# A planner's dependence between matmuls of one sum, and its figures for transfers, in a fused attention and expert kernel

## The chip, the cores and the metric

One core of a Trainium2 chip runs the whole program in one launch. The metric is the device time of an execution in microseconds (us), lower being better. The figure for a kernel is the median of its runs.

## The reference, cut to what matters

Three stages follow each other: attention that keeps the 32 largest scores of a row, a dense mixture of four experts, and a gated product of two linear maps. All is float32.

```python
# q, k, v: (2, 8, 576, 64)
scores = q @ k.T / sqrt(64)
kth    = 32nd largest of each row of scores
attn   = softmax(where(scores >= kth, scores, -1e9))
x      = (attn @ v) as (1152, 512)
p      = domain_probs / (sum(domain_probs) + 1e-9)          # (1152, 4)
x      = sum over e of p[:, e] * (relu(x @ w1[e]) @ w2[e])   # w1 512x1024, w2 1024x512
out    = ((x @ w_a) * (x @ w_b)) @ w_out                     # 512x1536, 1536x512
```

## The kernel before, in words

**Tiles and groups.** The 1152 rows make nine tiles of 128 rows (the ninth mixes the last 64 rows of both batches). They are taken in four groups of 1, 2, 3 and 3 tiles (`SIZES`). A group passes attention in four pairs of heads, so attention has 36 steps, one for a tile and a pair. In a step TensorE makes the scores of two heads, ScalarE copies them out (L821), VectorE finds the 32 largest with four `max` and three `match_replace` passes for each head (L842, L850), POOL and ScalarE turn them into weights (L867 to L892), TensorE transposes these (`weigh`, `turn`) and, after the last tile of the pair, multiplies by v. ScalarE and VectorE write the result into `xs` (L984, L986) as a rounded part and a remainder.

**Experts.** The first group goes through `plain` in full float32. The others go through `experts`: `first` makes one 128-wide piece of the hidden layer as a sum of four steps, one for each pair of heads (`a`), `second` one tile of the output as a sum over hidden pieces. A step is three matmuls, since operands are split in two parts. Each step is an operation of its own that names the step before it as `last`. Sums of `first`, of `second` and of `plain` use three banks of PSUM (`ms`). ScalarE and VectorE empty a hidden piece (L1077, L1081), and VectorE adds an expert's output (L1106). Weights come by loads of 512 KB (L518 is the line of all loads); ScalarE rounds them (L1007), POOL or VectorE makes the remainder (L1008).

**Gated stage.** `combine` makes sums of quarters of x, and `gated` does the three products, in the way of Strassen, with sums that are one operation each (`product`), emptied by L1387.

**q's halves.** From the second group on, `queries` splits q in two parts and transposes both at once. Each half of the partitions then holds one part; ScalarE copies that out (L726), and two DMAs within SBUF fetch the other half into `qb` (`big<-big`). For groups with the mixed tile, `qm` is filled in the same way (L736, `qm<-qm`).

**The order of work.** Nothing in the source fixes the order. `Plan.add` collects operations with an engine, an estimated duration (`hold`), a `lag` until others can see its end, a key, operations to wait for and tiles. `order` plays the program forward on a clock: each engine takes the ready operation with the lowest key whose tiles have a slot. It gives the instruction order of every engine, the DMA queue on SyncE (SP) included. `best` does so 42 times with random lateness added, replays every order in `rerun` with other random lateness, and keeps the order with the lowest mean. Only this order goes into the program; on the chip each engine runs its list in order and waits on semaphores for what an instruction really needs. Keys put scores, then attention, ahead of expert work, which is numbered from 1000 upwards in the order of the source.

In `order` an operation that ends is seen 45 ns later by others, and 130 ns later by TensorE (`SEEN`, `SEEN_PE`); TensorE's own `lag` is 165 ns (`tensor`). A load counts as landed after `ISSUE` 500 ns, its bytes at 320 bytes a ns on one shared line (`GBS`), and `LAND` ns.

Of the kernel before, what the change touches and what calls it, by code (L numbers as in the profile page):

```python
# [9 lines left out]
F32 = mybir.dt.float32  # L10
# [79 lines left out]
SEEN, SEEN_PE = 45, 130  # L90
COLD, COLD_END = 1.7, 46e3

OTHER = {"DVE": "POOL", "POOL": "DVE"}
RATES = {"DVE": 0.65, "POOL": 0.5}


def contend(engine, hold, other, left):
# [1 line left out]
    a, b = RATES[engine], RATES[other]  # L99
    t = min(hold / a, left / b)  # L100
    return t + hold - a * t, t + left - b * t
ISSUE, LAND, GBS, LANES = 500, 2100, 320.0, 8

# [5 lines left out]
class Plan:  # L111
# [37 lines left out]
    def rerun(self, got, draw):  # L149

        free, end, dma, users = {}, {}, 0.0, {}
        last, runs = 0.0, {}
        for op in got:
            t = free.get(op.engine, 0.0)
            for w in op.waits:
                t = max(t, end[id(w)] + (SEEN_PE if op.engine == "PE" else SEEN))

            for b in op.tiles:
                u = users.get(id(b))
                if u is None:  # L160
                    u = users[id(b)] = [max([self.freed.get(k, 0.0) for k in b.slots.cells(b.slot)] or [0.0])]
                t = max(t, u[0] + (SEEN_PE if op.engine == "PE" else SEEN))
            hold = op.hold * COLD if op.engine == "PE" and t < COLD_END else op.hold
            if op.engine == "SP":
                free["SP"] = t + ISSUE
                dma = max(dma, t + ISSUE) + op.nbytes / GBS
                e = dma + LAND + draw.uniform(0.0, LATE_DMA)
            else:
                if op.port:
                    other = OTHER[op.engine]  # L170
                    y = runs.get(other)
                    if y is not None and free[other] > t:
                        hold, left = contend(op.engine, hold, other, free[other] - t)
                        end[id(y)] += t + left - free[other]
                        free[other] = t + left
                if op.engine in OTHER:
                    runs[op.engine] = op if op.port else None
                free[op.engine] = t + hold
                e = t + hold + op.lag + (draw.uniform(0.0, LATE_ENGINE) if op.engine != "PE" else 0.0)
            end[id(op)] = e  # L180
            last = max(last, e)
            for b in op.tiles:
                k = (b.slots.name, b.slot)
                self.freed[k] = max(self.freed.get(k, 0.0), e)
        self.freed.clear()
        return last

    def order(self):
# [12 lines left out]
        late, ready, free, events, tick = {}, {}, {}, [], 0  # L201
# [16 lines left out]
        queue, now, done = [(op.since, -1, None) for op in self.ops if op.since], 0.0, []  # L218
# [28 lines left out]
        def pick(engine):  # L247
# [6 lines left out]
            while ready_:  # L254
                item = heapq.heappop(ready_)
                op = item[2]

                y = runs.get(OTHER[engine]) if BLOCK and op.port else None
                ok = y is None or free[y.engine] <= now
# [15 lines left out]
        while len(done) < len(self.ops):  # L275
            moved = False
            for engine in free:
                if free[engine] > now:
                    continue
                if engine == "SP" and len(lanes) >= LANES and lanes[-LANES] > now:  # L280
                    continue
                op = pick(engine)
                if op is None:
                    continue
                moved = True
                for t in op.tiles:
                    if t.slot is None:
                        t.slot = place(t)
                        t.slots.free.discard(t.slot)
                        t.slots.next += 1  # L290
                op.start = now
                done.append(op)
                if engine == "SP":
                    free[engine] = now + ISSUE
                    dma_free = max(dma_free, now + ISSUE) + op.nbytes / GBS
                    end = dma_free + LAND
                    lanes.append(end)
                else:
                    hold = op.hold * COLD if engine == "PE" and now < COLD_END else op.hold
                    if op.port:  # L300
                        other = OTHER[engine]
                        y = runs.get(other)
                        if y is not None and free[other] > now:
                            hold, left = contend(engine, hold, other, free[other] - now)
                            y.fin += now + left - free[other]
                            free[other] = now + left
                            heapq.heappush(queue, (y.fin, y.n, y))
                            heapq.heappush(queue, (free[other], -1, None))
                    if engine in OTHER:
                        runs[engine] = op if op.port else None  # L310
                    free[engine] = now + hold
                    end = now + hold + op.lag + op.late
                op.fin = end
                heapq.heappush(queue, (end, op.n, op))
                heapq.heappush(queue, (free[engine], -1, None))
            if moved:
                continue
            if not queue:
                raise RuntimeError("the plan stands still: " + str([(o.n, o.engine, o.key) for o in self.ops if o.start is None][:8]))
            now = max(now, queue[0][0])  # L320
            while queue and queue[0][0] <= now:
                _, _, op = heapq.heappop(queue)
                if op is None:
                    continue
                if isinstance(op, Buffer):
                    op.slots.free.add(op.slot)
                    continue
                if op.fin > now:
                    continue
                for t in op.tiles:  # L330
                    t.users -= 1
                    if not t.users:
                        heapq.heappush(queue, (now + t.slots.rest, -2 - op.n - 0.1 * op.tiles.index(t), t))
                for a in op.after:
                    a.left -= 1
                    a.at = max(a.at, now + (SEEN_PE if a.engine == "PE" else SEEN))
                    if not a.left:
                        heapq.heappush(late[a.engine], (a.at, a.n, a))
                        heapq.heappush(queue, (a.at, -1, None))
# [37 lines left out]
def body(tc, q, k, v, probs, w1, w2, wa, wb, wo, out):  # L377
# [58 lines left out]
    qm = const("qm", [128, 2, 2, 2, 128], F32R)  # L436
# [78 lines left out]
    def load(dst, src, key, after=(), tiles=(), nbytes=1 << 18, since=0.0):  # L515


        op = plan.add("SP", 0, lambda: nc.sync.dma_start(out=dst(), in_=src()), key, after, tiles, nbytes=nbytes)  # L518
        op.since = since
        return op  # L520
# [182 lines left out]
    def queries(pair, n, key, eng, rqv, tiles, lds):  # L703
# [3 lines left out]
        qa, qb, at = qas.tile(n), qbs.tile(n), atts.tile(key + 0.04)  # L707
# [8 lines left out]
        def turn():  # L716
# [6 lines left out]
        w = m * 128  # L723
        av = lambda: qa.ap[:, 0:2 * w].rearrange("p (j n) -> p j n", j=2)
        bv = lambda: qb.ap[:, 0:2 * w].rearrange("p (j n) -> p j n", j=2)
        e = scalar(2 * w, lambda: nc.scalar.activation(av(), at.ap[:, :, 0:w], AF.Copy), -901, [o], [at, qa])  # L726
        got = [e] + [
            load(lambda r=r: bv()[r * 64:(r + 1) * 64].bitcast(F32), lambda r=r: av()[(1 - r) * 64:(2 - r) * 64].bitcast(F32), -500, [e], [qa, qb], 512 * w)
            for r in range(2)
        ]  # L730
        pair.qd, pair.q = {0: got, 1: got}, [qa, qb]
# [1 line left out]
        if m < T:  # L733
            es_ = [
                scalar(
                    2 * REM, lambda b=b: nc.scalar.activation(  # L736
                        qm[:, :, b, 0, b * REM:(b + 1) * REM], at.ap[:, :, w + b * REM:w + (b + 1) * REM], AF.Copy
                    ), -900, [o] + qm_read[0] + qm_read[1], [at],
                ) for b in range(B)
            ]  # L740
            qm_read[:] = [], []
            pair.md = es_ + [
                load(lambda r=r: qm[r * 64:(r + 1) * 64, :, :, 1].bitcast(F32), lambda r=r: qm[(1 - r) * 64:(2 - r) * 64, :, :, 0].bitcast(F32), -400, es_, (), 1 << 17)
                for r in range(2)
            ]

# [707 lines left out]
    for i in range(FILL):  # L1454
        late = i >= 9
        op = tensor(
            120 if late else 215, lambda: mm(idle.ap[:, 0:256], zeros_[:, 0:128], zeros_[:, 128:384], start=True, stop=True),
            1e9 + i, [blank], [idle],
        )
# [33 lines left out]
```

## Time and profile before

| what | value |
|---|---|
| median of 3 runs | 823.16 us (821.83 to 823.45) |
| the profiled execution's own time | 820.39 us |
| its span, first to last instruction | 818.6 us |
| mean granted TensorE clock | 0.997 |
| busy TensorE (PE) / weight loads (PEld) | 789.1 / 705.0 us |
| busy VectorE (DVE) | 735.3 us |
| busy ScalarE (ACT) / GpSimd (POOL) | 525.0 / 350.7 us |

Busy time is a share of the whole span and hides stages. A matmul's recorded end is modelled and reaches into the next one, so that a mean duration is longer than the distance between starts; the distance of starts is the pace.

### The profile page before, as it was taken

The numbers are of one execution on the slowest core, as the hardware profiler recorded it, in microseconds if no ns is written. First come the engines' busy times: TensorE is split into PE (matmuls) and PEld (weight loads), VectorE is DVE, ScalarE is ACT, GpSimd is POOL, SyncE is SP. The second block draws the span as 40 slices with busy tenths as digits, with TensorE's granted clock in tenths as the row PEclk, the third lists the DMA queues.
The fourth block names the chain that finished last, engine by engine and source line by source line (L and its number), as shares of the span: only waits on it lengthen the run. The fifth ranks groups of instructions, "written<-read, shape, count | busy, mean of one in ns | idle before, by whom it ended". The sixth has DMA issues, their size and how long they took to land.

```text
span 818.6 us, 14468 instructions
## 1 busy us (share of the span) xinstructions
PE 789.1 (96%) x5221; PEld 705.0 (86%) x5221; DVE 735.3 (90%) x1447; ACT 525.0 (64%) x917; POOL 350.7 (43%) x317
## 2 busy tenths in 40 slices
PE   7589999999999999999999999999999999999997
PEld 6467777789899999899999999899989989899996
DVE  7999999999999999999984998888877899997654
ACT  6877887998899989888565667666634533341110
POOL 3524433798898967754121211221313333422120
PEclk9999999999999999999999999999999999999999
DMA  6839988856657462633334555989330412221013
GB/s 209 284 108 318 322 274 236 256 166 213 204 173 205 148 202 91 201 103 104 103 103 155 168 171 181 330 309 316 120 104 24 133 52 103 78 78 52 1 52 116
DMA packets 95511, 134.39 MB, mean 164 GB/s; under 512 B 11344, under 2 KB 69712, under 8 KB 93904
## 3 DMA queue, kind: packets, MB, share of 16 engines
q1 hardware_dynamic: 95440, 133.47, 51.1%
q8 instruction: 41, 0.67, 0.3%
q14 instruction: 30, 0.25, 0.1%
HBM read 115.36 MB, written 13.37 MB: 157 GB/s over the span
## 4 chain that ended last, share of the span: by engine, by line
PE 64%; DVE 26%; ACT 4%; DMA 3%; issue 1%; POOL 1%; SPq 0%; POOLq 0%; ACTq 0%
PE ps L536 61%; DVE low L842 12%; DVE low L850 10%; PE ps L539 2%; DMA raw<-in_moe_w_dram 1%; DVE mid L1081 1%; DMA big<-big 1%; DVE low L1106 1%; DMA low<-in_k_dram 1%; ACT low L892 1%; ACT mid L1007 0%; ACT lowa L821 0%; ACT low L881 0%; DVE rest L1387 0%; POOL low L877 0%
## 5 line engine op out<-in xcount | busy, mean ns | idle before, releaser
L536 PE MATMUL ps<-mid 128*128 128x512 f32 x1092 | 278.4, 394 | 0.0
L536 PEld LDWEIGHTS ps<-mid 128*128 128x128 f32 x1092 | 198.5, 188 | 32.8 <-DVE mid L1081 0.7
L536 PE MATMUL ps<-xs,mid 128*128 128x384 f32 (+1 forms) x1152 | 204.3, 321 | 1.2 <-DVE mid L1081 1.1
L536 PEld LDWEIGHTS ps<-xs,mid 128*128 128x128 f32 x1152 | 185.0, 189 | 9.9 <-DVE mid L1081 2.2
L842 DVE MAX8 low<-low 128x8 f32<-128x576 f32 x216 | 155.0, 749 | 0.1
L1298 POOL TENSOR_TENSOR low<-low 128x512 int32<-128x512 int32 x36 | 52.7, 1464 | 162.1 <-DVE low L1295 119.4
L1008 POOL TENSOR_TENSOR mid<-raw,mid 128x1024 fp32r<-128x1024 f32 x48 | 115.2, 2406 | 8.0 <-ACT mid L1007 6.9
L1007 ACT ACTIVATE mid<-raw 128x1024 fp32r<-128x1024 f32 x96 | 101.7, 1063 | 17.7 <-PE ps L536 16.5
L877 POOL TENSOR_TENSOR low<-lowa,low 128x576 f32<-128x576 f32 x70 | 98.8, 1430 | 29.4 <-ACT low L873 28.4
L850 DVE MATCH_REPLACE8 low<-low 128x576 f32<-128x576 f32 x144 | 106.3, 744 | 0.0
L536 PE MATMUL ps<-xs,big 128*128 128x320 f32 (+1 forms) x576 | 87.8, 297 | 0.1
L536 PEld LDWEIGHTS ps<-xs,big 128*128 128x128 f32 x576 | 81.3, 190 | 2.5 <-DVE low L1387 0.3
L536 PE MATMUL ps<-lowa_again,big 128*128 128x320 f32 (+1 forms) x432 | 66.8, 297 | 1.0 <-ACT rest L1396 0.8
L536 PEld LDWEIGHTS ps<-lowa_again,big 128*128 128x128 f32 x432 | 61.5, 190 | 3.4 <-ACT rest L1396 1.1
L1008 DVE TENSOR_TENSOR mid<-raw,mid 128x1024 fp32r<-128x1024 f32 x48 | 58.9, 1229 | 6.0 <-ACT mid L1007 5.7
L1077 ACT ACTIVATE mid<-ps 128x384 fp32r<-128x384 f32 (+1 forms) x96 | 43.3, 456 | 30.4 <-PE ps L536 27.8
L892 ACT ACTIVATE low<-low 128x576 f32<-128x576 f32 x70 | 51.1, 773 | 16.3 <-DVE low L889 16.1
L539 PE MATMUL ps<-identr,low 128*128 128x128 f32 x360 | 53.4, 283 | 7.3 <-ACT low L892 6.6
L873 ACT ACTIVATE low<-lowa,low 128x576 f32<-128x576 f32 x70 | 52.1, 776 | 11.8 <-POOL low L867 11.8
L539 PEld LDWEIGHTS ps<-identr,low 128*128 128x128 f32 x360 | 42.3, 144 | 19.2 <-ACT low L892 13.4
L1081 DVE SCALAR_TENSOR_TENSOR mid<-ps,mid 128x384 fp32r<-128x384 f32 (+1 forms) x96 | 48.2, 506 | 11.3 <-ACT mid L1077 10.8
L881 ACT ACTIVATE low<-low 128x576 f32<-128x576 f32 x70 | 54.6, 781 | 3.1 <-POOL low L877 3.1
(120 smaller groups left out, 1176.4 us busy)
## 6 DMA issues: line engine op xcount, KB each, us to landing
raw<-in_moe_w_dram SPq DMA_DIRECT2D x122, 512.0 KB, 3.9
big<-kscr SPq DMA_DIRECT2D x20, 576.0 KB, 6.0
low<-in_v_dram SPq DMA_DIRECT2D x24, 256.0 KB, 4.0
low<-in_moe_w_b_dram SPq DMA_DIRECT2D x12, 512.0 KB, 3.7
low<-in_moe_w_a_dram SPq DMA_DIRECT2D x12, 512.0 KB, 4.2
low<-in_moe_w_out_dram SPq DMA_DIRECT2D x12, 512.0 KB, 4.4
wscr<-big SPq DMA_DIRECT2D x6, 1024.0 KB, 7.4
mid<-wscr SPq DMA_DIRECT2D x6, 1024.0 KB, 5.2
```

Source lines behind the costliest of these rows:

```text
L536: nc.tensor.matmul(out, l, r, **kw)
L539: nc.tensor.transpose(out, a, i)
L842: 62 + 1.04 * width, lambda at=at, cs=cs: nc.vector.max(m8v()[:, x, cs], at()), key + 0.02 * r, [done],
L850: lambda at=at, cs=cs: nc.vector.match_replace(out=src[1](), in_to_replace=m8v()[:, x, cs], in_values=at(), imm_value=LOW),
L873: S, lambda x=x, s=s: nc.scalar.activation(ev(x), s.ap, AF.Relu, bias=endv()[:, x, 1:2], scale=-STEEP),
L877: pool_(S), lambda x=x, s=s: nc.gpsimd.tensor_tensor(ev(x), s.ap, ev(x), op=ALU.subtract), ks, [a], [s, ep]
L881: lambda x=x: nc.scalar.activation(ev(x), ev(x), AF.Exp, bias=endv()[:, x, 0:1], scale=scale, accum_out=sums.ap[:, x:x + 1]),
L892: S, lambda x=x: nc.scalar.activation(ev(x), ev(x), AF.Copy, scale=sums.ap[:, x:x + 1]),
L1007: hi = scalar(1024, lambda: nc.scalar.activation(u.ap[:, 0:1024], r.ap, AF.Copy), 500 + s, [ld], [u, r], sbuf=True)
L1008: sub = lambda eng: eng.tensor_tensor(u.ap[:, 1024:2048], r.ap, u.ap[:, 0:1024], op=ALU.subtract)
L1081: lambda h=h, p=p: nc.vector.scalar_tensor_tensor(h.ap[:, n:2 * n], p.ap[:, 0:n], 0.0, h.ap[:, 0:n], op0=ALU.max, op1=ALU.subtract),
L1298: return gpsimd(pool_(512), lambda: nc.gpsimd.tensor_tensor(t().bitcast(I32), fold(c.ap.bitcast(I32)), fold(lowv().bitcast(I32)), op=ALU.a ...
```

## The change

The planner alone changes; operations, tiles, keys and durations stay. In `order`, when a TensorE operation is placed, TensorE operations that wait for it count it as done at once (they can start when the engine is free), and its end no longer tells them; in `rerun` a TensorE operation no longer waits for another TensorE operation's end. `LAND` goes from 2100 to 2700 ns. The bytes that the planner counts for the exchange of q's halves double, for `qb` and for `qm`. `CHAIN` is read nowhere.

```diff
+CHAIN = True
-ISSUE, LAND, GBS, LANES = 500, 2100, 320.0, 8
+ISSUE, LAND, GBS, LANES = 500, 2700, 320.0, 8
...
             for w in op.waits:
-                t = max(t, end[id(w)] + (SEEN_PE if op.engine == "PE" else SEEN))
+                if w.engine != "PE" or op.engine != "PE":
+                    t = max(t, end[id(w)] + (SEEN_PE if op.engine == "PE" else SEEN))
...
                 op.start = now
                 done.append(op)
+                if engine == "PE":
+                    for a in op.after:
+                        if a.engine == "PE":
+                            a.left -= 1
+                            a.at = max(a.at, now)
+                            if not a.left:
+                                heapq.heappush(late["PE"], (a.at, a.n, a))
...
                 for a in op.after:
+                    if a.engine == "PE" and op.engine == "PE":
+                        continue
                     a.left -= 1
...
-            load(lambda r=r: bv()[r * 64:(r + 1) * 64].bitcast(F32), lambda r=r: av()[(1 - r) * 64:(2 - r) * 64].bitcast(F32), -500, [e], [qa, qb], 512 * w)
+            load(lambda r=r: bv()[r * 64:(r + 1) * 64].bitcast(F32), lambda r=r: av()[(1 - r) * 64:(2 - r) * 64].bitcast(F32), -500, [e], [qa, qb], 1024 * w)
...
-                load(lambda r=r: qm[r * 64:(r + 1) * 64, :, :, 1].bitcast(F32), lambda r=r: qm[(1 - r) * 64:(2 - r) * 64, :, :, 0].bitcast(F32), -400, es_, (), 1 << 17)
+                load(lambda r=r: qm[r * 64:(r + 1) * 64, :, :, 1].bitcast(F32), lambda r=r: qm[(1 - r) * 64:(2 - r) * 64, :, :, 0].bitcast(F32), -400, es_, (), 1 << 18)
```

## Rows read from the trace of the kernel before

**Rows 1.** By stretch: length, busy us of PE, PEld, DVE, ACT, POOL, then clock.
```profile
0.00:60.00 60.00, 44.09 (x282) 36.19 (x283) 54.18 (x121) 44.56 (x91) 23.69 (x42) 0.97 0.63 198
60.00:160.00 100.00, 93.89 (x688) 73.20 (x687) 99.89 (x218) 79.65 (x145) 44.62 (x49) 1.00 0.91 278
160.00:293.00 133.00, 131.77 (x1023) 119.32 (x1022) 131.57 (x285) 120.13 (x216) 117.80 (x84) 1.00 0.62 192
...
420.00:600.00 180.00, 180.00 (x979) 163.30 (x978) 150.59 (x236) 110.34 (x168) 38.13 (x26) 1.00 0.63 211
600.00:640.00 40.00, 38.97 (x256) 36.32 (x255) 32.55 (x72) 19.46 (x37) 9.81 (x10) 1.00 0.16 53
```

**Rows 2.** TensorE's instructions in order of time, around 293 us.
```profile
292.92 0.62 PE L539 MATMUL ps<-identr,big 128*128 128x128 f32 x6
293.38 1.82 PE L536 MATMUL ps<-xs,mid 128*128 128x384 f32 x9
```

**Rows 3.** VectorE's instruction that completes the third group's x.
```profile
293.08 0.56 DVE L986 TENSOR_TENSOR xs<-ps,xs 128x384 fp32r<-128x384 f32 x1
```

**Rows 4.** TensorE's instructions in order of time, from 477.8 to 488 us.
```profile
477.80 5.40 PE L536 MATMUL ps<-mid 128*128 128x512 f32 x23
483.04 0.69 PE L536 MATMUL ps<-xs,mid 128*128 128x384 f32 x3
483.56 0.86 PE L536 MATMUL ps<-mid 128*128 128x512 f32 x3
484.25 0.70 PE L536 MATMUL ps<-xs,mid 128*128 128x384 f32 x3
```

**Rows 5.** Who waited for whom, TensorE's matmuls and weight loads, whole span.
```profile
PE ps L536 <- DMA big<-big: 2.9, 3, 1.3
PE ps L536 <- DVE mid L1081: 1.1, 3, 0.4
PEld ps L536 <- DMA big<-big: 3.8, 4, 1.5
PEld ps L536 <- DVE mid L1081: 2.9, 8, 0.6
PEld ps L536 <- DMA raw<-in_moe_w_dram: 0.8, 2, 0.5
```

**Rows 6.** All engines in order of time, one exchange of q's halves.
```profile
149.75 0.82 ACT L726 ACTIVATE big<-ps 128x768 fp32r<-128x768 f32 x1
...
150.60 1.11 SPq L518 DMA_DIRECT2D big<-big  x2
...
156.20 1.17 PE L536 MATMUL ps<-big 128*128 128x288 f32 x7 [1.28 <-DMA big<-big]
```

**Rows 7.** DMA issues: what, count, KB each, median us from issue to landing.
```profile
raw<-in_moe_w_dram SPq DMA_DIRECT2D x122, 512.0 KB, 3.9
...
big<-big SPq DMA_DIRECT2D x16, 128.0 KB, 6.7
...
big<-big SPq DMA_DIRECT2D x8, 192.0 KB, 5.7
```

**Rows 8.** All engines in order of time, the start.
```profile
8.49 0.63 ACT L591 ACTIVATE big<-low 128x512 fp32r<-128x512 f32 x1 [0.72 <-DMA low<-in_k_dram]
...
9.03 0.63 ACT L821 ACTIVATE lowa<-ps 128x576 f32<-128x576 f32 x1
...
9.69 1.50 DVE L842 MAX8 low<-lowa 128x8 f32<-128x576 f32 x2 [2.16 <-ACT lowa L821]
```

**Rows 9.** VectorE's evictions, whole span: count, busy us, mean ns, idle before.
```profile
L1081 DVE SCALAR_TENSOR_TENSOR mid<-ps,mid 128x384 fp32r<-128x384 f32 (+1 forms) x96 | 48.2, 506 | 11.3 <-ACT mid L1077 10.8
L1106 DVE SCALAR_TENSOR_TENSOR low<-ps,pr,low 128x512 f32<-128x512 f32 x44 | 32.6, 743 | 6.1 <-PE ps L536 5.9
```

**Rows 10.** The same groups from 160 to 293 us.
```profile
L1081 DVE SCALAR_TENSOR_TENSOR mid<-ps,mid 128x256 fp32r<-128x256 f32 x31 | 12.7, 414 | 0.4 <-ACT mid L1077 0.3
L1106 DVE SCALAR_TENSOR_TENSOR low<-ps,pr,low 128x512 f32<-128x512 f32 x14 | 10.4, 742 | 0.0
```

## The prediction

> **What bounds the kernel now.** I read the busy time by stretch first [rows 1]. TensorE (PE) is the bound after about 160 us: from 420 to 600 us it is busy all 180.00 us, while VectorE (DVE) has 29 us to spare. Over the whole span it is busy for 789.1 of 818.6 us, so there are 29.5 us in which it stands still, and their places matter: 60.00 - 44.09 = 15.9 us lie before 60 us, 100.00 - 93.89 = 6.1 us between 60 and 160, 133.00 - 131.77 = 1.2 us between 160 and 293, and 1.0 us between 600 and 640. Most of the rest is the tail behind the last matmul. The granted clock is 0.97 before 60 us and 1.00 in the other stretches listed, so the clock has nothing to give.
>
> The early idle time is not TensorE's own fault. DVE, which searches the 32 largest scores, is busy 99.89 of 100 us from 60 to 160 and 131.57 of 133 from 160 to 293 [rows 1]. The two engines meet at 293 us: DVE's L986 begins at 293.08 and writes the last part of the second expert stage's x [rows 3], and TensorE's expert matmuls go on at 293.38 [rows 2]. Before that point time is set by DVE and by the chain from it through ScalarE and TensorE; behind it by TensorE's work. So a change of order can win only TensorE's stalls behind some 150 us, and whatever makes DVE begin or run earlier. It can lose on either engine.
>
> **The change, part by part.** *The removed wait.* The 165 + 130 = 295 ns between two steps of one sum are the planner's. The chip never waited them, so removing them takes nothing from the program by itself: 0. What changes is the order. The old planner left a sum for 295 ns and took a step of another sum. The rows show this: three matmuls of 384 columns, three of 512, and so on [rows 4]. The pace says what this costs. Twenty-three matmuls of 512 in a run start over 483.04 - 477.80 = 5.24 us, 228 ns each, so three take 0.68 us. The alternating pair takes 484.25 - 483.04 = 1.21 us, of which the 384s take 0.52 (483.04 to 483.56) and the 512s 0.69. Alternating costs at most 0.01 us for three matmuls. With 1092 matmuls of 512, were all of them alternated, the whole would be 364 x 0.01 = 3.6 us; many stand in runs already, so I take 0 and keep 0 to -3.6 for the range.
>
> *Sums that end one after the other.* Two alternating sums end nearly together; run back to back, the first ends one sum earlier and its hidden piece can be emptied while the second runs. TensorE waited 1.1 us in 3 places for L1081, and weight loads 2.9 us in 8 [rows 5]. I take half of the first, -0.5; bounds 0 and -2.9.
>
> *q's exchange.* Copied out by L726 from 149.75 to 150.57, the two DMAs are issued at 150.60, and TensorE's scores wait for them until 156.20, 1.28 us of it idle [rows 6]. The old figures put the landing of a three-tile exchange at 1000 + 614 + 2100 = 3.7 us behind the first issue; the new ones at 1000 + 1229 + 2700 = 4.9; the row shows 5.6. In the median, landings are 6.7 and 5.7 us behind the issue [rows 7]. The planner will put some 1.2 us of other work ahead of such scores. TensorE's waits of this kind are 2.9 us in 3 places [rows 5]. I count the 1.28 as 1.2 won, 0.4 for the remaining ones behind 160 us, and nothing for the ones before, where DVE sets the pace: -1.6; bounds 0 and -3.8, the weight loads' whole waiting. The scores do not come later than before, since they cannot start before the landing anyway; the cover is expert work that is ready. Without it the wait returns: 0.
>
> *The landing of other loads.* A 512 KB load is planned with 500 + 1638 + 2100 = 4.2 us, now 4.8, and the median is 3.9 [rows 7]. So for weights the new figure is further off. ScalarE takes up a load 0.6 us later in the planner's eyes; what is queued behind it there is put ahead of it. TensorE waited for a weight load only 0.8 us in all [rows 5], and weights stay a unit ahead of use, so I take 0; bounds 0 and +0.8. The Trainium skill ("DMA: Bandwidth & Descriptors", the fixed and variable cost of a DMA) gives about 2.0 us plus bytes over 436 GB/s; by that rule a half of q takes some 2.5 us and the old figure was the right one, so the change would move the plan away from the chip. The rows disagree for the exchange, at 5.7 and 6.7 us, and the measurement decides there.
>
> *The start.* ScalarE waits 0.72 us for a load of k, rounds it at 8.49, and only then copies out the first scores at 9.03; DVE's first search starts at 9.69 [rows 8]. With a later landing in the plan, the scores may be put first: at most 9.03 - 8.49 = 0.54 us, all of it on DVE's path. I take -0.3; bounds 0 and -0.54, or +0.5 if the later landing puts filler matmuls or key work in front of the first scores.
>
> *Sum.* 0 - 0.5 - 1.6 + 0 - 0.3 = -2.4 us. Against the profiled execution's 820.39 (818.6 of span and 1.8 around it) this gives 818.0; the median of the runs shown is 823.16, 2.8 above that execution, so I forecast 823.16 - 2.4 = **820.8 us**. A measurement of this kernel can tell about 0.2%, 1.6 us, the width of the three runs.
>
> **The rivals.** *Nothing measurable.* All 42 drawn orders are new, so small stalls go and others come; the 2.4 us are worth little against them. For it: TensorE idles only 1.2 us in the 133 us before 293 [rows 1]. Against it: the named waits are real. Time 823.2, give or take 1.6.
>
> *DVE stands in front of evictions that come late.* This one ends slower. The 295 ns were also a reserve in the plan. Without them the planned TensorE runs ahead of the chip's, evictions L1081 and L1106 are put earlier in DVE's list, and DVE, which keeps its order, waits there with top-32 passes behind it; POOL, ScalarE and in the end TensorE wait for those. The place is 160 to 293 us, where DVE is full. Over the whole span DVE waits 11.3 + 6.1 us ahead of 96 + 44 evictions [rows 9], but between 160 and 293 only 0.4 us ahead of 31 + 14 [rows 10]. The others thus cost (17.4 - 0.4) / 95 = 0.18 us each. If half of the 45 cost as much in the full stretch, that is +4.0 us: 827.2. It decides once it is over the 2.4 won. For it: DVE has nothing in reserve there. Against it: evictions wait for the same matmuls, and a sum run in one go ends earlier.
>
> *The longer landing misplaces loads.* If loads really land 0.6 to 0.9 us before the plan has them, ScalarE and POOL do later what could be done earlier, and the third group's x comes later by about that at one or two places: +1.8 us, 825.0. For it: 3.9 against 4.8 [rows 7]. It is what the Trainium skill's rule (same page and section) would make of the change. Against it: engines before 293 are full of other work.
>
> *The order hardly changes.* The constants are read by every plan, and the rows show alternation that must go, so I give this no share of its own apart from "nothing measurable".
>
> **How the numbers follow.** Forecast 0.45, nothing measurable 0.26, DVE in front of late evictions 0.22, misplaced loads 0.07. The first gives faster 0.45, the second same 0.26, the last two slower 0.29. The forecast's own range is 816.0 (823.16 less 3.8, 2.9 and 0.5, the ends of the three terms that I count) to 821.5. The slower cases reach from 824.8 to 828.0 (the 827.2 and 0.8 for weights). Signs are mixed, so the range takes in both: 816.0 to 828.0. Beyond it lie all 45 late evictions (8.1 us), a gain from the pace as well, and what I have not seen; I leave 2 in 10 to these.
>
> **What would show it.** Right: runs of six or more matmuls of one kind in place of alternating threes; TensorE's wait for `big<-big` falling from 2.9 us to about 1; its wait for L1081 falling; the first search at 9.2 to 9.7; the x of the third group complete at 293 or before, and TensorE's idle time behind 160 us below 3 us. Wrong: DVE idle between 160 and 293 us above the present 1.4, with L1081 or L1106 behind the wait; expert matmuls of the third group held beyond 293.4; new TensorE waits that outweigh the old ones. If TensorE's stalls shrink before 293 and the end does not move, DVE's path was the bound for longer than I think.

## The result, and the profile after

The changed kernel takes 814.74 us in the median of 4 runs (814.30 to 815.28), the one before beside it 822.72 (821.83 to 823.45): a ratio of 0.9904, 95% interval 0.9887 to 0.9921. Faster, as forecast, but by 8.0 us in place of 2.4, and outside of the range. The two profiled executions are only 820.39 - 815.06 = 5.3 us apart, since that of before lay below the four runs beside it; it is near the 820.6 to 821.3 us that the same kernel had in five later sessions. In one of these the pair stood at 814.53 and 821.34, 0.9918 (0.9903 to 0.9933), so about 6.8 us.

Busy time by stretch in the kernel after, columns as in [rows 1]:

```profile
0.00:60.00 60.00, 43.58 (x279) 36.55 (x279) 54.78 (x122) 43.95 (x90) 22.26 (x41) 0.97 0.64 193
60.00:160.00 100.00, 96.19 (x703) 75.91 (x703) 98.45 (x215) 80.12 (x146) 48.34 (x51) 1.00 0.91 287
160.00:293.00 133.00, 130.78 (x1025) 119.28 (x1026) 132.13 (x287) 122.51 (x220) 115.52 (x83) 1.00 0.62 190
...
420.00:600.00 180.00, 180.00 (x993) 164.31 (x992) 155.81 (x236) 108.58 (x167) 34.98 (x25) 1.00 0.63 206
600.00:640.00 40.00, 38.16 (x247) 35.45 (x246) 35.55 (x73) 21.86 (x41) 12.37 (x11) 1.00 0.24 77
```

TensorE is idle for 3.8 us from 60 to 160, where it was 6.1, but for 2.2 us from 160 to 293, where it was 1.2, and for 1.8 from 600 to 640, where it was 1.0. Over the whole span the idle time is 813.3 - 784.3 = 29.0 us against 29.5 before. So, net, 4.8 of the 5.3 us are inside of the busy time. The first line of the page after:

```profile
PE 784.3 (96%) x5221; PEld 705.9 (87%) x5221; DVE 740.8 (91%) x1447; ACT 524.4 (64%) x917; POOL 351.9 (43%) x317
```

It is the same 5221 matmuls as before, busy for 789.1 us then. A recorded end reaches some 0.16 us past the next start ([rows 4]: 477.80 + 5.40 against 483.04), so a matmul that starts 100 ns late leaves no idle time. To see such losses I took the distance between successive starts and subtracted the usual pace of the shape (229 ns for 512 columns, 174 for 384, 120 for 256, and so on). Call it standing time. Its level depends on the paces chosen; both kernels run the same matmuls, so the differences hardly do:

| stretch, us | before | after | difference |
|---|---|---|---|
| 0 to 60 | 30.8 | 32.1 | +1.3 |
| 60 to 160 | 12.2 | 8.7 | -3.5 |
| 160 to 280 | 4.7 | 2.9 | -1.9 |
| 280 to 300 | 0.6 | 2.1 | +1.5 |
| 300 to 440 | 3.1 | 1.1 | -2.1 |
| 440 to 600 | 0.5 | 0.0 | -0.5 |
| 600 to the end | 2.2 | 2.0 | -0.2 |

Before rounding the differences add up to -5.3 us, the whole difference of the profiled executions. The order on TensorE has changed as the edit says. Its instructions after, in order of time, answer to [rows 4]; its list now has 521 stretches of like instructions, where it had 715:

```profile
446.50 8.07 PE L547 MATMUL ps<-xs,mid 128*128 128x384 f32 x45
454.42 8.36 PE L547 MATMUL ps<-mid 128*128 128x512 f32 x36
462.62 4.35 PE L547 MATMUL ps<-xs,mid 128*128 128x384 f32 x24
```

The pace in a run is 8.20 / 36 = 228 ns for 512 columns, as before. Behind 60 us the mean distance over all 1091 matmuls of 512 columns whose successor is recorded went from 232.0 to 231.5 ns, and over the 768 of 384 from 176.5 to 176.0. That is 0.5 + 0.4 = 0.9 us. The scores made from `big` (288 columns) give more: behind 60 us their mean distance went from 167.9 to 151.6 ns, 3.4 us over 208 matmuls. Most of that is the wait for the exchange of q's halves, which stood before 160 us. TensorE's matmuls of before, waits from 60 to 293 us:

```profile
PE ps L536 <- DMA big<-big: 2.4, 2, 1.3
```

Around the third group's x, first TensorE's first matmuls of its expert stage before, then TensorE's instructions after (compare [rows 2]) and VectorE's (compare [rows 3]):

```profile
282.92 0.69 PE L536 MATMUL ps<-xs,mid 128*128 128x384 f32 x3
```

```profile
279.56 3.29 PE L547 MATMUL ps<-xs,mid 128*128 128x384 f32 x18
...
284.64 1.64 PE L550 MATMUL ps<-identr,low 128*128 128x128 f32 x13 [1.35 <-ACT low L903]
...
292.33 2.86 PE L547 MATMUL ps<-xs,mid 128*128 128x384 f32 x15
```

```profile
292.35 0.54 DVE L997 TENSOR_TENSOR xs<-ps,xs 128x384 fp32r<-128x384 f32 x1
```

TensorE comes to this place earlier: 18 matmuls of the second expert stage have started by 282.7, where before the first one starts at 282.92. Then it waits 1.35 us for attention's weights (L903 is L892 of before). That x is complete at 292.89, before at 293.64. From there to the start of the last matmul it is 515.3 us, before 519.8. So of the 5.3 us only 0.8 are an earlier x; the rest lies behind it, where by the paces TensorE has some 1.7 us less work left and stands some 2.8 us less.

The waits, those of [rows 5] that are left (whole span; there is none for `big<-big` and none for `raw<-in_moe_w_dram`):

```profile
PE ps L547 <- DVE mid L1092: 0.3, 1, 0.3
```

The exchange of q's halves that [rows 6] showed, after, and the median landings, compare [rows 7]:

```profile
149.77 0.81 ACT L737 ACTIVATE big<-ps 128x768 fp32r<-128x768 f32 x1 [0.15 <-PE ps L550]
150.99 1.11 SPq L529 DMA_DIRECT2D big<-big  x2
...
162.91 0.70 PE L547 MATMUL ps<-big 128*128 128x288 f32 x4
```

```profile
big<-big SPq DMA_DIRECT2D x16, 128.0 KB, 6.2
...
big<-big SPq DMA_DIRECT2D x8, 192.0 KB, 7.3
```

The halves take 6 to 7 us still; the scores that need them start 12 us behind the issue, with other work in front. The start, compare [rows 8] (L832 is L821, L602 is L591, L853 is L842):

```profile
8.36 0.65 ACT L832 ACTIVATE lowa<-ps 128x576 f32<-128x576 f32 x1 [0.70 <-PE ps L547]
8.90 0.62 ACT L602 ACTIVATE big<-low 128x512 fp32r<-128x512 f32 x1
9.04 0.76 DVE L853 MAX8 low<-lowa 128x8 f32<-128x576 f32 x1 [1.55 <-ACT lowa L832]
```

The scores are copied out ahead of the load's rounding, and the first search starts at 9.04 in place of 9.69.

### The profile page after: what moved, and what is told of

The parts are those of the page before. It is cut to its first block, busy times and chain, and to the rows that moved or that the text cites. A ratio compares the mean times of both kernels' runs of the same rounds, so it can differ in the third digit from the quotient of the medians.

```text
span 813.3 us, 14483 instructions
## 1 busy us (share of the span) xinstructions
PE 784.3 (96%) x5221; PEld 705.9 (87%) x5221; DVE 740.8 (91%) x1447; ACT 524.4 (64%) x917; POOL 351.9 (43%) x317
## 4 chain that ended last, share of the span: by engine, by line
PE 81%; DVE 10%; issue 3%; ACT 2%; POOL 2%; DMA 1%; POOLq 0%
PE ps L547 76%; DVE low L853 5%; PE ps L550 4%; DVE low L861 4%; DMA raw<-in_moe_w_dram 1%; POOL mid L1019 1%; POOL low L888 1%; ACT low L903 1%; DVE rest L1398 0%; ACT low L892 0%; ACT lowa L961 0%; POOL rest L1401 0%; ACT lowa L832 0%; POOL big L606 0%; DVE low L1283 0%
## 5 line engine op out<-in xcount | busy, mean ns | idle before, releaser
L547 PE MATMUL ps<-mid 128*128 128x512 f32 x1092 | 261.8, 392 | 0.2 <-POOL mid L1019 0.2
L547 PEld LDWEIGHTS ps<-mid 128*128 128x128 f32 x1092 | 201.7, 188 | 39.5 <-POOL mid L1019 0.5
L547 PE MATMUL ps<-xs,mid 128*128 128x384 f32 (+1 forms) x1152 | 190.7, 320 | 0.3 <-DVE mid L1092 0.3
L547 PEld LDWEIGHTS ps<-xs,mid 128*128 128x128 f32 x1152 | 180.9, 189 | 2.8 <-DVE mid L1092 0.5
L853 DVE MAX8 low<-low 128x8 f32<-128x576 f32 x216 | 154.5, 746 | 0.0
L1019 DVE TENSOR_TENSOR mid<-raw,mid 128x1024 fp32r<-128x1024 f32 x48 | 62.1, 1298 | 8.9 <-ACT mid L1018 8.4
L903 ACT ACTIVATE low<-low 128x576 f32<-128x576 f32 x70 | 51.5, 777 | 15.9 <-DVE low L900 15.8
L550 PE MATMUL ps<-identr,low 128*128 128x128 f32 x360 | 51.4, 280 | 9.6 <-ACT low L903 8.7
L892 ACT ACTIVATE low<-low 128x576 f32<-128x576 f32 x70 | 54.5, 780 | 4.5 <-POOL low L888 4.4
L1401 POOL TENSOR_TENSOR low<-low 128x256 f32<-128x256 f32 (+1 forms) x30 | 29.7, 991 | 60.2 <-DVE low L1398 59.0
```

Of the source, the lines that this page charges most:

```text
L547: nc.tensor.matmul(out, l, r, **kw)
L550: nc.tensor.transpose(out, a, i)
L853: 62 + 1.04 * width, lambda at=at, cs=cs: nc.vector.max(m8v()[:, x, cs], at()), key + 0.02 * r, [done],
L892: lambda x=x: nc.scalar.activation(ev(x), ev(x), AF.Exp, bias=endv()[:, x, 0:1], scale=scale, accum_out=sums.ap[:, x:x + 1]),
L903: S, lambda x=x: nc.scalar.activation(ev(x), ev(x), AF.Copy, scale=sums.ap[:, x:x + 1]),
L1019: sub = lambda eng: eng.tensor_tensor(u.ap[:, 1024:2048], r.ap, u.ap[:, 0:1024], op=ALU.subtract)
```

## The experiments

A ratio is to the kernel before, run in the same session, where it had 820.6 to 821.3 us (822.7 beside after). "Arrival" is the end of the instruction that completes the third group's x, "distance" the time from there to the start of the last matmul, both from one profiled execution. That execution can lie some way from its kernel's median: 2.5 us above it in land and chain_q, 2.2 above in chain_land, 2.2 below in figures. Arrivals of these are to be read with that.

| kernel | ratio (95% interval) | arrival | distance | TensorE's wait for `big<-big` |
|---|---|---|---|---|
| before (profile above) | 1 | 293.6 | 519.8 | 2.9 |
| before_s100 | 0.9990 (0.9977 to 1.0003) | 294.8 | 518.8 | 1.8 |
| before_s200 | 1.0001 (0.9992 to 1.0011) | 295.2 | 519.7 | 1.3 |
| land | 1.0013 (0.9995 to 1.0030) | 299.0 | 517.8 | none |
| qbytes | 1.0009 (0.9996 to 1.0022) | 296.7 | 518.9 | 2.7 |
| figures | 1.0036 (1.0025 to 1.0046) | 295.5 | 519.1 | none |
| chain | 1.0020 (1.0009 to 1.0032) | 298.7 | 517.1 | 3.5 |
| chain_s100 | 1.0024 (1.0009 to 1.0039) | 297.6 | 516.9 | 3.4 |
| chain_s200 | 0.9965 (0.9951 to 0.9979) | 296.3 | 513.6 | 1.7 |
| chain_q | 1.0013 (1.0003 to 1.0023) | 301.6 | 516.0 | 0.7 |
| chain_land | 0.9977 (0.9957 to 0.9997) | 297.2 | 517.2 | 0.2 |
| after | 0.9904 (0.9887 to 0.9921) | 292.9 | 515.3 | none |
| after_again | 0.9918 (0.9903 to 0.9933) | 292.3 | 515.4 | none |
| after_s100 | 0.9963 (0.9950 to 0.9976) | 295.2 | 515.6 | 1.8 |
| after_s200 | 0.9961 (0.9948 to 0.9974) | 294.4 | 515.4 | none |
| after_s300 | 0.9944 (0.9927 to 0.9961) | 294.0 | 515.4 | none |
| after_o168 | 0.9946 (0.9931 to 0.9961) | 293.9 | 515.2 | none |
| after_dve | 0.9965 (0.9952 to 0.9978) | 296.9 | 515.3 | none |
| after_pe | 0.9959 (0.9945 to 0.9973) | 295.0 | 515.3 | none |
| after_dve_late | 0.9956 (0.9941 to 0.9971) | 293.0 | 517.9 | none |

### The parts, one at a time

**chain**: the edits of `order` and `rerun` without the figures.

```diff
 # after, with
-ISSUE, LAND, GBS, LANES = 500, 2700, 320.0, 8
+ISSUE, LAND, GBS, LANES = 500, 2100, 320.0, 8
-... [e], [qa, qb], 1024 * w)
+... [e], [qa, qb], 512 * w)
-... es_, (), 1 << 18)
+... es_, (), 1 << 17)
```

> The change without its figures: TensorE's successors in one sum are free at once (order and replay), LAND 2100, exchange bytes as before. Sums theory (sums in one go bring most of the 8 us): 814 to 818 us, and 60 to 160 us with TensorE busy over 95.5 us. Figures theory (landing figures bring most): 821 to 824 us. Draw theory (any new order moves the time by several us, whatever is edited): anything from 814 to 826, and the parts do not add up to the whole.

**land**: before, with `LAND` 2700.

```diff
-ISSUE, LAND, GBS, LANES = 500, 2100, 320.0, 8
+ISSUE, LAND, GBS, LANES = 500, 2700, 320.0, 8
```

> Before, with LAND 2700 alone. Sums theory: 821 to 824 us. Figures theory: 817 to 820 us, the first search on VectorE some 0.5 us earlier than 9.69. Draw theory: anything from 814 to 826.

**qbytes**: before, with `1024 * w` and `1 << 18`.

```diff
-... [e], [qa, qb], 512 * w)
+... [e], [qa, qb], 1024 * w)
-... es_, (), 1 << 17)
+... es_, (), 1 << 18)
```

> Before, with the doubled bytes of the exchange of q's halves alone. Sums theory: 821 to 824 us. Figures theory: 819 to 822 us, TensorE's wait for big<-big under 2.9 us. Draw theory: anything from 814 to 826.

**figures**: before, with the edits of land and qbytes together.

> Before, with LAND 2700 and the doubled bytes, without the edit for sums. Sums theory: 820 to 824 us, sums still alternate. Figures theory: 814 to 818 us. Draw theory: anything from 814 to 826; together with the chain kernel, the two gains do not sum to 8.

No part gains alone in these orders: 1.0020, 1.0013, 1.0009 and 1.0036, of which land and qbytes cannot be told from 1. The sums and figures theories both fall as to time, and the parts' effects add up with the wrong sign. The draw theory allowed anything and is left. Each part is one draw here, and land, qbytes and figures were tried with no other, so an unlucky draw is not excluded for them. Two things can be read all the same. First, the profile of chain shows where its gain is lost. TensorE around the third group's x, and VectorE's instruction that completes it:

```profile
283.60 0.60 PE L550 MATMUL ps<-identr,low 128*128 128x128 f32 x4
286.29 1.06 PE L550 MATMUL ps<-identr,low 128*128 128x128 f32 x4 [2.09 <-DVE xs L1224]
288.71 1.12 PE L550 MATMUL ps<-identr,low 128*128 128x128 f32 x4 [1.35 <-ACT low L903]
```

```profile
298.11 0.56 DVE L997 TENSOR_TENSOR xs<-ps,xs 128x384 fp32r<-128x384 f32 x1 [1.28 <-ACT xs L995]
```

It waits 2.09 and 1.35 us there and the x arrives 5 us later than before, which undoes a distance 2.7 us shorter. The earlier part of the sums theory's sign did come: from 60 to 160 us TensorE is busy for 95.50 us in chain (93.89 before; land 92.15, figures 93.47). Standing time, as a difference from before, says the same of all profiles but those with added costs. From 60 to 160 us it is -0.5 to +2.8 us in the five other orders without the edit for sums, and -0.7 to -5.7 in the eleven profiles with it. From 280 to 300 us it is -0.1 to +0.8 without the edit. It is +4.9 to +8.2 in all five kernels of the table that have the edit without both figures, and +1.5 to +3.1 with the whole change (+5.6 in after_s100). So in these profiles sums in one go win TensorE time early and lose some of it again shortly before the third group's x, most where a figure is missing. Second, with `LAND` 2700 alone the wait for `big<-big` is gone, and in each profile that I looked at the start's order goes with `LAND`: first scores before the load's rounding with 2700 (land, figures, after), behind it with 2100 (before, before_s100, before_s200, qbytes, chain, chain_s100, chain_q). The start in figures:

```profile
7.85 0.65 ACT L821 ACTIVATE lowa<-ps 128x576 f32<-128x576 f32 x1 [0.20 <-PE ps L536]
8.40 0.62 ACT L591 ACTIVATE big<-low 128x512 fp32r<-128x512 f32 x1
8.53 0.76 DVE L842 MAX8 low<-lowa 128x8 f32<-128x576 f32 x1 [1.13 <-ACT lowa L821]
```

Neither made these kernels faster. In land TensorE even stands 2.8 us more than before from 60 to 160 us, although the exchange's waits are gone.

### Other draws of the planner's lateness

```diff
-            draw = random.Random(r)
+            draw = random.Random(100 + r)      # 200 + r, 300 + r
```

> The whole change, with other random lateness in the planner's 42 tries (seeds from 100 on). Together theory (sums in one go and larger figures gain only together, and gain in any draw): a ratio of 0.985 to 0.995, as the changed kernel's 0.990. Draw theory (the changed kernel is a lucky draw): a ratio of 0.996 to 1.008, the gain gone.

> The whole change, seeds from 200 on. Together theory: a ratio of 0.985 to 0.995. Draw theory: a ratio of 0.996 to 1.008, and some 0.3 percent or more away from the one with seeds from 100 on.

> The kernel before, seeds from 100 on. Together theory: a ratio of 0.997 to 1.004, above both changed kernels with other seeds. Draw theory: anywhere from 0.990 to 1.010, among the changed ones.

> The kernel before, seeds from 200 on. Together theory: a ratio of 0.997 to 1.004. Draw theory: anywhere from 0.990 to 1.010, and some 0.3 percent or more away from the one with seeds from 100 on.

The kernel before does not gain by another draw (0.9990, 1.0001), the whole change does (0.9963, 0.9961). By the ranges on record these two ratios are the draw theory's; but their intervals end at 0.9976 and 0.9974, so the gain is not gone. Both theories hold a part: the change gains in each draw tried, and its first draw is a good one. The draws of the whole change are not independent. In `best` the first try has no lateness at all, and later tries keep the early part of the best order so far. With seeds from 0, 200 and 300 on, TensorE's first 1333 of 5221 matmuls are the same; the lists of POOL and of SP are the same with seeds from 200 and from 300 on. Only seeds from 100 on gave a plainly different order (the 330th matmul is already another).

**chain_s100** and **chain_s200** make the same edit to chain.

> The edit for sums alone (figures as before), seeds from 100 on. Arrival theory (sums in one go shorten what TensorE has left after the third group's x by 2.5 to 4.5 us in any draw; when that x arrives is a draw, 293 to 299 us): the distance from the arrival to the last matmul 515 to 517.5 us, the arrival anywhere in 292 to 299, the ratio 0.993 to 1.002. Together theory (without the larger figures the arrival is late, as in the first chain kernel): arrival near 298 us, ratio 1.000 to 1.004.

> The edit for sums alone, seeds from 200 on. Arrival theory: 515 to 517.5 us from the arrival to the last matmul, the arrival anywhere in 292 to 299, and 1 us or more from the arrivals with the other seeds. Together theory: arrival near 298 us, ratio 1.000 to 1.004.

Distances are 516.9 and 513.6 (the second below the expected 515 to 517.5), arrivals 297.6 and 296.3. The distance is shorter in every order with sums in one go (513.6 to 517.2 in five, against 517.8 to 519.8 in six without the edit). A part of this goes with the later arrival and not with the edit: without it, too, the latest x has the shortest distance (land, 299.0 and 517.8). The arrivals of chain's three seeds, 296.3 to 298.7, are behind those of before's three, 293.6 to 295.2. That fits the together theory; it does not show it, since land and qbytes are as late without the edit. The ratio of chain_s200, 0.9965, contradicts that theory: with the old figures it gains as much as after_s100 with the new ones. It is the arrival theory's; chain_s100's 1.0024 fits the other. These draws are not independent either: chain and chain_s100 have the same list of POOL, and the same first 319 matmuls.

### A cost that the planner is not told

**after_dve** repeats maxima on VectorE, **after_dve_late** the same at step 34, **after_pe** repeats scores on TensorE.

```diff
 # after_dve (after_dve_late: n == 34)
-lambda at=at, cs=cs: nc.vector.max(m8v()[:, x, cs], at())
+lambda at=at, cs=cs, w=3 if n == 20 and r == rounds - 1 else 1: [nc.vector.max(m8v()[:, x, cs], at()) for _ in range(w)]
 # after_pe
-            for c in range(2):
+            for c in [0, 1] * (4 if n == 22 else 1):
```

> The changed kernel with the last max of step 20's two heads made three times, which the planner is not told: 4 more maxima of 0.66 us, 2.6 us on VectorE at some 232 us. If VectorE's path to the third group's x sets the end (arrival theory): that x arrives 2 to 2.6 us later than 292.9, the end moves by as much, 816.7 to 817.4 us where the changed kernel has 814.7. If TensorE's work sets it: under 815.7.

> The changed kernel with step 22's scores made four times, which the planner is not told: 24 more matmuls of 288 columns, 0.133 us each, 3.2 us on TensorE at some 240 us. If VectorE's path sets the end: TensorE's standing still of 2 us at 280 to 300 us takes up some of it, and the time is 814.7 plus 0.5 to 1.8. If TensorE's work sets it: plus 3.2, 817.9.

> The changed kernel with the last max of step 34's two heads made three times: the same 4 maxima, 2.6 us, but at some 405 us, behind the third group's x. Arrival theory: VectorE has time to spare there, the end moves by under 0.8 us (ratio 0.989 to 0.993). If VectorE's work sets the end anywhere: 2.6 us or more (ratio 0.993 to 0.996).

after_dve costs 817.77 - 814.53 = 3.2 us by the medians (of two sessions), 4.0 in the arrival and in the last matmul's start, more than the 2.6 added; at 817.77 it is a little above the 816.7 to 817.4 expected. after_pe costs 2.7 by the medians and 2.2 in the last matmul's start (810.37 against 808.17); its arrival is 2.1 us later too, and its standing time from 280 to 300 us is the 2.1 us of the changed kernel, nothing of it taken up. Its 817.26 lies between the two expected times. after_dve_late costs 3.2 by the medians and 2.8 in the profile, with the arrival where it was. So the arrival theory falls in its strict form: added time on either engine, before the x or behind it, moved the end. The expectation for after_dve_late was also wrong about its place: VectorE has no time to spare there. The changed kernel, columns as in [rows 1]:

```profile
293.00:420.00 127.00, 127.00 (x906) 117.17 (x905) 126.90 (x255) 101.59 (x183) 64.07 (x56) 1.00 0.43 128
```

The rows of after_dve_late show the way. VectorE's instructions in order of time, then weight loads' waits from 380 to 440 us:

```profile
409.35 2.35 DVE L853 MAX8 low<-low 128x8 f32<-128x576 f32 x3
411.61 1.21 DVE L1019 TENSOR_TENSOR mid<-raw,mid 128x1024 fp32r<-128x1024 f32 x1
412.74 0.55 DVE L1092 SCALAR_TENSOR_TENSOR mid<-ps,mid 128x384 fp32r<-128x384 f32 x1
413.20 2.34 DVE L853 MAX8 low<-low 128x8 f32<-128x576 f32 x3
415.46 0.54 DVE L1092 SCALAR_TENSOR_TENSOR mid<-ps,mid 128x384 fp32r<-128x384 f32 x1
```

```profile
PEld ps L547 <- DVE mid L1092: 2.0, 3, 0.9
```

The evictions L1092 stand in VectorE's list behind the longer maxima, and TensorE's next step needs them; in the changed kernel no weight load waits for L1092 in this stretch. The same wait is in after_dve, weight loads from 236 to 262 us:

```profile
PEld ps L547 <- DVE mid L1092: 2.1, 1, 2.1
```

In these three runs, each with its cost inside attention, time that the plan does not know went to the end through whichever wait came first. Nothing was added behind 420 us, where VectorE does have time to spare.

### Which figure the sums need, and how far the draw goes

chain_land is chain with `LAND` 2700, chain_q chain with the doubled bytes; after_o168 has `ORDERS` 168 in place of 42.

> The edit for sums with LAND 2700, bytes of the exchange as before. If LAND is what sums in one go need (TensorE's wait for big<-big was gone in each kernel with LAND 2700 but one): wait under 1 us, third group's x at 292 to 296 us, ratio 0.990 to 0.997. If the bytes are needed: x at 296 to 299, ratio 0.997 to 1.003. Draw theory: either.

> The edit for sums with doubled bytes of the exchange, LAND 2100. If LAND is needed: the wait for big<-big 1.5 us or more, third group's x at 296 to 299 us, ratio 0.997 to 1.003. If the bytes are needed: wait under 1 us, x at 292 to 296, ratio 0.990 to 0.997.

> The changed kernel with 168 tries in place of 42, the order with the lowest replayed mean kept. If the planner's own figure tells good draws from bad: a ratio of 0.986 to 0.991. If it does not, at this size: 0.991 to 0.997, as the draws with other seeds.

chain_q is as slow as chain (1.0013), with the latest arrival of all, 301.6, as expected if `LAND` is needed; its wait for `big<-big`, 0.7 us, is what was expected if the bytes are. chain_land gains 0.23% (0.9957 to 0.9997), with that wait at 0.2 us, but its ratio is outside of the 0.990 to 0.997 expected, and its x arrives at 297.2, in a profiled execution 2.2 us above the median, not at 292 to 296. So it is a hint that `LAND` helps the sums, and no more: one draw each, and chain_s200 gains more with neither figure. Four times as many tries gave 0.9946, no better than other seeds: the planner's own figure did not find a better order at this size.

**after_again** is the changed kernel unchanged, **after_s300** a fourth draw.

> The changed kernel as it is, beside the kernel before in a new session. If the 1 percent is the kernel's: a ratio of 0.989 to 0.992. If the kernel before was 2 us slow in the first comparison: 0.992 to 0.996, at or near the other draws' 0.9946 to 0.9963, so that the first draw is no lucky one.

> The whole change, seeds from 300 on. Together theory: a ratio of 0.993 to 0.998, as with seeds from 100 and 200 on, and 515 to 517 us from the third group's x to the last matmul. Draw theory: outside of that.

The 0.9918 is a little above the first ratio, with intervals that overlap, and its arrival and distance repeat to 0.6 and 0.1 us. The kernel before had been 1.4 to 2.1 us higher beside the first one than in the five later sessions. Seeds from 300 on give 0.9944 and a distance of 515.4, as the together theory expected; as said, that order is nearly the one with seeds from 200 on. No version tried beats the changed kernel.

## Why the prediction was wrong in size

**What it had right.** The removed wait is the planner's alone and alternating costs nearly nothing: 0.9 us at most, inside of 0 to -3.6. The exchange: TensorE's wait for `big<-big` fell from 2.9 us to none. The larger figures take it away (none in land and figures; 1.8 us in after_s100, though). The start: ScalarE's order turned as described, and the search began 0.65 us earlier, a little past the bound of 0.54. That value also moves by itself: with the changed kernel's plan it was 9.0, 9.2, 9.2, 9.5 and 8.5 in five profiles, and from 0 to 60 us TensorE stood 1.3 us longer, so no gain from it can be seen. The wait for L1081 fell from 1.1 to 0.3. Runs of one kind replaced the threes. The x was complete before 293. The slow rival did not come about in the changed kernel. Its evictions from 160 to 293 us, compare [rows 10]:

```profile
L1092 DVE SCALAR_TENSOR_TENSOR mid<-ps,mid 128x256 fp32r<-128x256 f32 x29 | 12.0, 413 | 1.3 <-ACT mid L1088 1.1
L1117 DVE SCALAR_TENSOR_TENSOR low<-ps,pr,low 128x512 f32<-128x512 f32 x14 | 10.3, 738 | 0.0
```

VectorE waits 1.3 and 0.0 us there, where it waited 0.4 and 0.0, and over the span 6.6 and 3.7, where [rows 9] had 11.3 and 6.1. One sign of being right did not come: TensorE's idle time behind 160 us, to be below 3 us, is 2.2 + 1.8 = 4.0 us in the two stretches shown above.

**The step that failed** is "a change of order can win only TensorE's stalls behind some 150 us", and with it the sum's terms "0" for the removed wait and "nothing for the ones before" 160. By starts, TensorE stands 3.5 us less from 60 to 160 and 1.9 less from 160 to 280; it gives 1.5 back before 300, when it has to wait for attention's weights, and wins 2.1 more until 440. Time won before 293 was not lost for want of an earlier x: TensorE put expert work there, and had less left behind. From 60 to 160 us, 2.4 of the 3.5 us are the two waits for the exchange, which the rows did show and of which I counted 1.2. Elsewhere I had read TensorE's losses off its idle time, and that could not show them: from 160 to 280 us idle time fell by 0.4 us (1.2 to 0.9) where standing time fell by 1.9. I had also taken the stretch before 293 us to belong to VectorE. The runs with unplanned costs show that it belongs to both: 2.6 us more on VectorE and 3.2 more on TensorE each moved the end by 2 to 4 us.

**A slip in the term for q's exchange.** The plan's new landing is not 4.9 us behind the first issue. `order` puts the bytes of the second half behind those of the first (`dma_free`), so it is 500 + 2 x 1229 + 2700 ns = 5.7 us, where the old plan had 500 + 2 x 614 + 2100 = 3.8. That is 1.8 us more cover, not 1.2, and it fits the 5.6 us of [rows 6]. The term itself, -1.6, is not shown by any run: land and figures lose the same waits and gain nothing.

**The sum was of the wrong form.** I added up parts. Measured in one draw each, the parts are +0.2%, +0.1%, +0.1% and together, in the first draw, -0.8 to -1.0%. With sums in one go but without both figures the third group's x came 3 to 8 us late, at 296.3 to 301.6, and with both it came at 292.3 to 295.2. That the parts need each other is the likely reading and not proven, since chain_s200 gains 0.35% without the figures. Over its four seeds the whole change has a mean ratio of (0.9911 + 0.9963 + 0.9961 + 0.9944) / 4 = 0.9945, or 4.5 us (0.9911 is the mean of the first seed's two measurements), with three of the four orders much alike. The first draw lies another 2.8 us below that mean, and as far as these draws tell that is luck. The mean would have been inside of the range, the draw was not, and a draw's spread of some 3 us was missing from the terms of the sum: "nothing measurable" was the only place where I had allowed for it.

**What stays open.** Why the third group's x comes late with sums in one go and the old figures. In chain and chain_s100 VectorE finishes that group's searches at 277.3 and 276.3 us, in the changed kernel at 273.4, before at 272.5; but after_s100 finishes at 277.0 and still has the x at 295.2, and chain_s200 finishes at 272.4 and has it at 296.3. No run here ties this to one wait. Whether the figures alone would gain in another draw was not tried. Nor was it tried whether `order` or `rerun` carries the edit's effect.

## What to carry to other kernels

Where a planner writes the order, repairing one of its figures can leave the time as it was or lengthen it (figures, +0.36%), and a change of the model is judged over several draws, with their spread beside it, and with a look at whether the draws are different orders at all. Idle time of TensorE hides losses shorter than the part of a matmul's record that reaches past the next start; distances between starts show them. Where two engines are both full, as here until 420 us, a stall seen on one is not free because the other "sets the pace": work that does not depend on the other can fill it.

## What the runs showed of the hardware that was not expected

The same plan began its first search on VectorE at 8.5 to 9.5 us in five executions, so that half a microsecond at the start is not evidence of a change. And 2.6 us of added maxima cost the end as much or more at both places in the profiles, 4.0 us at some 236 us and 2.8 at some 410, although VectorE's busy time from 420 to 600 us leaves 24 of 180 us free: what counted was what stood directly behind them in its list.
